# Feed-forward weights in alternating pieces, loaded one piece further ahead, with the low parts of the first layer formed on GpSimd

## The chip, the core and the metric

The kernel runs on one core of a Trainium2 chip. The metric is device time in microseconds (us). In the rows PE is TensorE's matmul, PEld its weight load, DVE VectorE, ACT ScalarE, POOL GpSimd, and SP SyncE, which only issues transfers.

## The reference: what is computed

An mLSTM recurrence over 768 steps for 4 batches of 8 sequences with head dimension 40, then a feed-forward layer in two matrix products with a piecewise activation between them:

```python
m_new = np.maximum(f_gate[:, :, t] + m, i_gate[:, :, t])        # per step t
f_stab = np.exp(f_gate[:, :, t] + m - m_new); i_stab = np.exp(i_gate[:, :, t] - m_new)
C = f_stab * C + i_stab * outer(v_t, k_t);  n = f_stab * n + i_stab * k_t
y[:, :, t] = sigmoid(o_gate_t) * (C @ q_t) / np.maximum(np.abs(n . q_t), 1.0)
# x: 3072 tokens x 320, the y of all batches and steps
h = x @ w_in                                                     # 320 x 2048
g = np.where(h >= 1, h, np.where(h <= -1, 0.0, (h + 1) ** 2 / 4))
out = g @ w_out                                                  # 2048 x 320
```

## The kernel before

The 768 steps are cut into 6 chunks of 128, so there are 24 heads of work n = 0 to 23 (a chunk of one batch, 8 sequences at once). Four heads make a group of 512 tokens. The feed-forward layer goes over six groups j = 0 to 5, and in each over 16 pieces fc of 128 of the 2048 inner features; call x = 16 j + fc the number of such a piece. `mm1(j, fc)` makes h of a piece in one bank `psh` (8 matmuls of 512 columns: high parts xh, wh against low parts xl, wl, since a product in fp32r keeps fewer bits), ScalarE and VectorE form r = g(h), and `mm2` multiplies r into four banks `pso`, two pieces (LAG) later. There are two `psh` banks, so mm1(x) cannot start before r of x-2 has been taken out of its bank.

While the layer runs over one group, the heads of the next are computed between its pieces: `prep` (select of the decay matrix Abc on GpSimd, its exponentials on ScalarE, v scaled by gates on GpSimd), `score` (products `psa<-raw`, multiplied into Abc on VectorE), `main` (products `psa<-C,qn` and `psa<-v,Abc`, the sums hv, the quotients z, sz and y on VectorE, `carry_on` with products `psa<-v,vk` for the next state C, a transposition `psa<-ident,y`, and the copies xh on ScalarE and xl, xh on VectorE that mm1 of the next group needs). The heads 0 to 3 go first, in a front part whose order is written out by hand in `STEPS`; their own `carry_on` (products `psa<-ow`, from v that GpSimd has scaled) follows during group 0.

The weights come as int64 words of float64 values and are converted during group 0. Each layer has 8 pieces, in_0 to in_7 and out_0 to out_7, each good for two values of fc. `load_w` brings one into a raw buffer `wraw` (transfers are all issued by SyncE, in order). `convert` runs `words` (mg on ScalarE; mg, the sign bits and the joining SCALAR_TENSOR_TENSOR on VectorE; the low half words on GpSimd) and, for in_i, `split`: wh on ScalarE (a cast), then wl = win - wh on VectorE. out_i is used as plain fp32 in group 0 (`pso<-ow,r`) and split in group 1 only. `win`, the converted piece of w_in, has one buffer.

What sets the order: `W_ORDER` lists the pieces, `DUE(fc)` says how many of them are converted by piece fc, `split_next` converts one, behind the instructions marked ("x", "act") and ("x", "dve"), which are the copies xh and xl of the last head done so far, and then loads the piece two places on. All else in this part is placed by the framework's scheduler, which follows these marks, the order in the program and the buffers; each engine then runs its list strictly in order.

Of the kernel before, what the change touches and what calls it, by code (L numbers as in the profile page):

```python
# [31 lines left out]

LAG = 2

PLAIN_FC = 16

# [10 lines left out]


GATES_AT = 34
DUE = lambda fc: 3 + fc

STEPS = (
# [3 lines left out]
)  # L61
# [37 lines left out]
def mlstm_ffn_kernel(ctx, tc, qk, qn, vk, og, fi0, fi, fib, w_in, w_out, cst, out):  # L99
    nc = Core(tc)  # L100
# [80 lines left out]
    mb = {}  # L181

    def load_batch():
        mb["row"] = mid.tile([NSEQ, 2, 4 * L], F32, name="fi_r")
        nc.sync.dma_start(mb["row"], fi[:, :, L:5 * L])
        mb["fi"] = mid.tile([P, 2, L], F32, name="fi_b")
        nc.sync.dma_start(mb["fi"], fib)
# [10 lines left out]

    def batch_sums():
        a, m = mb["fi"][:, 0, :], mb["m"]  # L200
        ah = mb["ah"] = mid.tile([P, L], F32, name="ah_b")
        ac = mb["ac"] = mid.tile([P, L], F32, name="ac_b")
        nc.vector.tensor_tensor(out=a, in0=a, in1=m[:, :L], op=ALU.add)
        nc.vector.tensor_tensor(out=a, in0=a, in1=m[:, 1:], op=ALU.subtract)
        nc.vector.tensor_scalar(out=ah, in0=a, scalar1=CLAMP, scalar2=GRID, op0=ALU.max, op1=ALU.add)
        nc.vector.tensor_scalar(out=ah, in0=ah, scalar1=-GRID, scalar2=None, op0=ALU.add)
        nc.vector.tensor_tensor_scan(out=ac, data0=rst, data1=ah, initial=0.0, op0=ALU.mult, op1=ALU.add)
        nc.sync.dma_start(a_d[1:5].rearrange("c s t -> (c s) t"), ac)
        nc.vector.scalar_tensor_tensor(out=a, in0=a, scalar=CLAMP, in1=ah, op0=ALU.max, op1=ALU.subtract)
# [160 lines left out]
    ol = {}  # L370
# [18 lines left out]
        nc.vector.scalar_tensor_tensor(out=out, in0=mg.bitcast(I32), scalar=3, in1=out,  # L389
                                       op0=ALU.logical_shift_left, op1=ALU.bitwise_or)  # L390

    def split(hi, lo, w):
        nc.scalar.copy(hi, w)
        yield
        nc.vector.tensor_tensor(out=lo, in0=w, in1=hi.bitcast(F32), op=ALU.subtract)

    raws = {}

    def load_w(kind, i):
        if kind == "in":  # L400
            n = 2 * P
            raw = stage.tile([P, 3, 2 * n], I32, name="wraw", bufs=2)
            at = nc.sync.dma_start(raw.rearrange("p k f -> p (k f)"), w_in[i])
        else:
            raw = stage.tile([P, 2, 2 * DM], I32, name="wraw", bufs=2)
            at = nc.sync.dma_start(raw.rearrange("p k f -> p (k f)"), w_out[i])
        raws[kind, i] = raw
        return at

    def convert(kind, i):  # L410
        raw = raws.pop((kind, i))
        if kind == "in":
            sl = slice(2 * i * P, 2 * (i + 1) * P)
            w = stage.tile([P, 3, 2 * P], F32, name="win", bufs=1)
            words(w, raw)
            yield
            yield from split(wh[:, :, sl], wl[:, :, sl], w)
        else:
            of[i] = ow.tile([P, 656], F32, name="ow")[:, :2 * DM].rearrange("p (k e) -> p k e", k=2)
            words(of[i], raw)  # L420
            if 2 * i >= PLAIN_FC:
                yield
                yield from split_out(i)

    def split_out(i):
        w = of.pop(i)
        ol[i] = ow.tile([P, 656], F32R, name="ow")[:, :2 * DM].rearrange("p (k e) -> p k e", k=2)
        yield from split(oh[:, 2 * i:2 * i + 2, :], ol[i], w)


    W_ORDER = [("in", 0)]
    for i in range(NFC // 2):
        if i + 1 < NFC // 2:
            W_ORDER.append(("in", i + 1))
        W_ORDER.append(("out", i))


    front = True
# [274 lines left out]
    for n in range(NS):  # L713
        j, r = divmod(n, NTC)
# [87 lines left out]
    for what in STEPS.split():  # L802
        n = int(what[1]) if what[1:2].isdigit() else 0
        hh = int(what[2:] or 0)
        if what == "Lg":
            first_gates()
        elif what == "Lf":
            load_batch()
        elif what == "Lc":
            nc.sync.dma_start(cs_t, cst[0:120, P:])  # L810
        elif what == "Li":
            nc.sync.dma_start(ident, cst[:, :P])
        elif what == "Lo":
            load_og(0)
        elif what[:2] == "Lq":
            load_qk(hh)
        elif what[:2] == "Lv":
            load_v2(hh)
        elif what[:2] == "Lw":
            mark["load"] = load_w(*W_ORDER[hh])  # L820
        elif what[0] == "s":
            score_mm(n)
        elif what[0] == "m":
            score_mul(n, hh)
        elif what[0] == "g":
            if n:
                batch_sums()
            else:
                run(gate_sums(n))
        elif what[0] == "b":  # L830
            batch_maxima()
        elif what[0] == "k":
            run(gate_tail(n))
        elif what[0] == "h":
            gate_exps(n)
        elif what[0] == "A":
            add_sums(n)
        elif what[0] == "E":
            exponents(n)
        elif what[0] == "p":  # L840
            first_sums()
        elif what[0] == "v":
            scale1(n)
        elif what[0] == "o":
            sigmoid(0)
        elif what[0] == "x":
            decay(n, hh)
        elif what[0] == "c":
            rest = convert(*W_ORDER[nw])
# [29 lines left out]
    for x in range(NG + LAG):  # L879
        j, fc = divmod(x, NFC)  # L880
        if x < NG:
            if j == 0:
                while nw < min(len(W_ORDER), DUE(fc)):
                    split_next()
                if nw == len(W_ORDER) and late is None:
                    stages.close()
                    late = ctx.enter_context(tc.tile_pool(name="late", bufs=1, side="right"))
            if fc == 0:
                ops[j] = [ps_o.tile([P, 512], F32, name="pso") for _ in range(NTC)]
            if j == 1 and fc % 2 == 0 and fc < PLAIN_FC:  # L890
                with tc.issue_after(mark["r", "act"].ins), tc.issue_after(mark["r", "dve"].ins):
                    for _ in split_out(fc // 2):
                        pass
            if x == GATES_AT:
                load_gates(later, NC - 1, NC)
                steps = gate_steps(NC - 1)
            if x >= GATES_AT:
                with tc.issue_after(mark["r", "dve"].ins):
                    next(steps, None)
            r = mm1(j, fc)  # L900
            if x == 0:
                with tc.issue_after(mark["r", "dve"].ins):
# [68 lines left out]
```

## Time and profile before

| | us |
|---|---|
| time, median of 3 runs (518.02 to 518.27) | 518.25 |
| span of the profiled execution, first to last instruction | 516.2 |
| time outside the span (median less span) | 2.05 |
| TensorE busy in the span | 490.7 |
| VectorE, ScalarE, GpSimd busy | 343.0, 289.1, 135.9 |
| mean granted TensorE clock | 0.979 |

The profiled execution is one of its own, with no device time noted beside its span; the difference of 2.05 us to the median is taken as what lies around the span. Group 0 runs in it from 33.6 us, when mm1(0) starts, to 143.0 us, when mm1(16) starts. From 160 us to the end TensorE is nearly always busy. A row of a view by stretches gives, for each engine, its busy time and in brackets its number of instructions; then the granted clock (1.00 is full, 0.50 half), the busy share of the transfer engines and what they moved. A busy time of TensorE at half clock is still busy: the loss stands in the column of the clock.

### The profile page before, as it was taken

Reading aid. Unit: us, or ns where it says so; the run is one execution under the profiler, and the core shown is the slowest. Engines: PE = TensorE matmul, PEld = TensorE weight load, DVE = VectorE, ACT = ScalarE, POOL = GpSimd, SP = SyncE. Lnnn points to the kernel's source line nnn. Section 1 sums busy time; section 2 is a strip of 40 time slices with the busy share of each in tenths; the row PEclk is TensorE's granted clock in tenths of the full one; section 3 lists DMA queues with packets and bytes.
Section 4 is the critical chain, followed back from the end, with each engine's and each line's share of the span. In section 5 each row is a group of like instructions: output and inputs, shape, how many; then the busy total and the mean of one; then the engine's idle time right before and its main releaser. Section 6 shows DMA issues by size and latency. Waiting matters only on the chain.

```text
span 516.2 us, 8817 instructions
## 1 busy us (share of the span) xinstructions
PE 490.7 (95%) x3396; PEld 419.4 (81%) x3399; DVE 343.0 (66%) x621; ACT 289.1 (56%) x560; POOL 135.9 (26%) x136
## 2 busy tenths in 40 slices
PE   8985999889898999999999998999999999999996
PEld 3763877778677989988889988889888889988986
DVE  4789896679758776759696657756756745444332
ACT  4525884436087555676645567555377554455553
POOL 2324531343433333323142314403230210000000
PEclk8987999979999999999999999999999999999999
DMA  8868664364441303323223423113522000010001
GB/s 227 257 183 307 161 189 138 115 193 150 131 146 40 107 27 96 118 66 111 65 78 83 133 80 118 68 53 96 170 81 77 16 1 1 0 52 1 1 2 51
DMA packets 29646, 51.48 MB, mean 100 GB/s; under 512 B 10060, under 2 KB 19940, under 8 KB 29604
## 3 DMA queue, kind: packets, MB, share of 16 engines
q1 hardware_dynamic: 29604, 50.92, 32.4%
q8 instruction: 27, 0.44, 0.4%
q14 instruction: 15, 0.12, 0.1%
HBM read 46.80 MB, written 4.04 MB: 98 GB/s over the span
## 4 chain that ended last, share of the span: by engine, by line
PE 85%; DVE 6%; ACT 5%; DMA 3%; issue 1%; SPq 0%; ACTq 0%; DVEq 0%
PE pso L82 33%; PE psh L82 33%; PE psa L82 15%; ACT Abc L82 1%; PE pso L85 1%; DMA raw<-in_qk 1%; ACT L82 1%; PE psa L85 1%; DVE ow L82 1%; DMA wraw<-in_w_in 1%; PE psh L85 1%; ACT r L82 1%; DVE win L82 1%; DMA out<-r 1%; ACT sig L82 0%
## 5 line engine op out<-in xcount | busy, mean ns | idle before, releaser
L82 ACT ACTIVATE r<-psh,half 128x512 f32<-128x512 f32 x96 | 65.4, 685 | 111.7 <-PE psh L82 111.4
L82 DVE SCALAR_TENSOR_TENSOR r<-psh,r 128x512 f32<-128x512 f32 x96 | 65.8, 686 | 71.5 <-ACT r L82 71.3
L82 PE MATMUL psh<-xh,wh 128*128 128x512 f32 x288 | 104.3, 418 | 6.7 <-DVE r L82 6.1
L82 PE MATMUL pso<-oh,gh 128*128 128x320 f32 x320 | 100.6, 317 | 2.4 <-ACT gh L82 2.1
L82 PE MATMUL psh<-xh,wl 128*128 128x512 f32 x288 | 99.8, 401 | 0.0
L82 PE MATMUL pso<-ow,gh 128*128 128x320 f32 x320 | 99.2, 312 | 0.0
L82 PE MATMUL pso<-oh,gl 128*128 128x320 f32 x320 | 94.0, 311 | 1.6 <-DVE gl L82 1.6
L82 DVE TENSOR_TENSOR gl<-r,gh 128x512 fp32r<-128x512 f32 x80 | 62.2, 779 | 40.5 <-ACT gh L82 40.4
L82 ACT CAST gh<-r 128x512 fp32r<-128x512 f32 x80 | 49.4, 618 | 51.0 <-DVE r L82 50.4
L82 PEld LDWEIGHTS pso<-oh,gh 128*128 128x128 f32 x320 | 60.1, 188 | 7.4 <-ACT gh L82 2.5
L82 PEld LDWEIGHTS psh<-xh,wl 128*128 128x128 f32 x288 | 55.2, 192 | 13.1 <-DVE wl L85 0.4
L82 PEld LDWEIGHTS psh<-xh,wh 128*128 128x128 f32 x288 | 51.8, 194 | 15.2 <-DVE r L82 6.8
L82 PEld LDWEIGHTS pso<-ow,gh 128*128 128x128 f32 x320 | 60.2, 188 | 2.8
L82 PE MATMUL psh<-xl,wh 128*128 128x512 f32 x192 | 62.3, 405 | 0.0
L82 ACT ACTIVATE r<-r 128x512 f32<-128x512 f32 x96 | 60.4, 632 | 2.5
L82 PEld LDWEIGHTS pso<-oh,gl 128*128 128x128 f32 x320 | 58.9, 188 | 2.1 <-DVE gl L82 1.9
L82 ACT ACTIVATE Abc<-Abc,nA 128x128 f32<-128x128 f32 x160 | 49.9, 391 | 0.2
L82 POOL TENSOR_TENSOR v<-vk,G 128x328 f32<-128x328 f32 x36 | 30.6, 856 | 58.3 <-issue 45.9
L82 PEld LDWEIGHTS psh<-xl,wh 128*128 128x128 f32 x192 | 36.8, 192 | 8.6
L82 PE MATMUL pso<-ow,r 128*128 128x320 f32 x128 | 38.5, 443 | 0.5 <-DVE ow L82 0.5
L82 POOL TENSOR_SCALAR_AFFINE_SELECT Abc<-Abc 128x1024 f32<-128x1024 f32 x20 | 25.4, 1275 | 48.3 <-DMA Abc<-a_d 46.1
L82 POOL TENSOR_TENSOR m<-m 128x1024 bf16<-128x1024 f32 x12 | 24.4, 2037 | 46.4 <-DVE m L82 46.4
(203 smaller groups left out, 681.0 us busy)
## 6 DMA issues: line engine op xcount, KB each, us to landing
Abc<-a_d SPq DMA_DIRECT2D x20, 512.0 KB
raw<-in_qk SPq DMA_DIRECT2D x48, 160.0 KB
vk<-in_vk SPq DMA_DIRECT2D x20, 324.0 KB
wraw<-in_w_in SPq DMA_DIRECT2D x8, 768.0 KB
wraw<-in_w_out SPq DMA_DIRECT2D x8, 640.0 KB
sig<-in_og SPq DMA_DIRECT2D x6, 640.0 KB
out<-r SPq DMA_DIRECT2D x24, 160.0 KB
qn<-in_qn SPq DMA_DIRECT2D x20, 180.0 KB
```

Source lines behind the costliest of these rows:

```text
L82: r = getattr(self.engine, name)(*args, **kwargs)
L85: r = getattr(self.engine, name)(*args, **kwargs)
```

## The change

Seven things change.

1. `W_ORDER` is in_0, out_0, in_1, out_1 and so on. Before it was in_0, in_1, out_0, in_2, out_1, ..., with the first layer one piece further ahead.
2. The raw buffers are three instead of two, and a conversion loads the piece three places on.
3. A new step Lw2 in the hand-written front loads the third piece, in_1, right after the constants `cs`. The two before it are in_0 and out_0 (before: in_0 and in_1), and the step c then loads out_1 (before: out_0).
4. wl is formed on GpSimd instead of VectorE (`split` takes the engine).
5. Only two pieces are converted ahead of mm1(0) instead of three. The later ones are converted after mm1 of their fc and behind the marks of r instead of those of xh and xl, with `DUE` one higher from fc = 1 on.
6. The tiles ah and ac of the gate sums for the chunks 1 to 4 lie in the space of the row buffer `fi_r`, which makes room for the third raw buffer.
7. `PLAIN_FC`, which was 16 (all pieces), is gone with the branches that it switched.

```diff
-DUE = lambda fc: 3 + fc
+DUE = lambda fc: 3 + fc + (fc > 0)
 STEPS = (
-    "Lg Li Lo Lq0 Lv0 Lq1 Lw0 Lf Lq2 Lv2 Lq3 Lw1 Lc o w9 E0 ...
+    "Lg Li Lo Lq0 Lv0 Lq1 Lw0 Lf Lq2 Lv2 Lq3 Lw1 Lc Lw2 o w9 E0 ...
...
-        mb["row"] = mid.tile([NSEQ, 2, 4 * L], F32, name="fi_r")
+        mb["all"] = mid.tile([P, 2, 4 * L], F32, name="fi_r")
+        mb["row"] = mb["all"][:NSEQ]
...
-        ah = mb["ah"] = mid.tile([P, L], F32, name="ah_b")
-        ac = mb["ac"] = mid.tile([P, L], F32, name="ac_b")
+        ah = mb["ah"] = mb["all"][:, 0, :L]
+        ac = mb["ac"] = mb["all"][:, 0, L:2 * L]
...
-    def split(hi, lo, w):
+    def split(hi, lo, w, eng):
         nc.scalar.copy(hi, w)
         yield
-        nc.vector.tensor_tensor(out=lo, in0=w, in1=hi.bitcast(F32), op=ALU.subtract)
+        eng.tensor_tensor(out=lo, in0=w, in1=hi.bitcast(F32), op=ALU.subtract)
...
-            raw = stage.tile([P, 3, 2 * n], I32, name="wraw", bufs=2)
+            raw = stage.tile([P, 3, 2 * n], I32, name="wraw", bufs=3)
...
-            yield from split(wh[:, :, sl], wl[:, :, sl], w)
+            yield from split(wh[:, :, sl], wl[:, :, sl], w, nc.gpsimd)
...
-    W_ORDER = [("in", 0)]
-    for i in range(NFC // 2):
-        if i + 1 < NFC // 2:
-            W_ORDER.append(("in", i + 1))
-        W_ORDER.append(("out", i))
+    W_ORDER = [(kind, i) for i in range(NFC // 2) for kind in ("in", "out")]
...
-            if nw + 2 < len(W_ORDER):
-                load_w(*W_ORDER[nw + 2])
+            if nw + 3 < len(W_ORDER):
+                load_w(*W_ORDER[nw + 3])
...
-                while nw < min(len(W_ORDER), DUE(fc)):
+                while nw < 2:
                     split_next()
...
             r = mm1(j, fc)
...
+            while j == 0 and nw < min(len(W_ORDER), DUE(fc)):
+                split_next("r")
```

How this moves the instructions is not to be seen in the diff. Three places follow; the number behind a name tells buffers apart, and only their order counts.

First, the transfers that SyncE issues in the front. `wraw` is a raw weight piece, `vk`, `qn` and `raw` (qk) belong to the heads 4 and 5, `m_b` carries the row maxima to the gate sums, and `Abc` is the decay matrix of a head, read back from `a_d`. Before:

```order
L85 DMA wraw_161<-in_w_in 128x1536
L85 DMA cs_99<-in_cst 120x369
L82 DMA vk_493<-in_vk 128x648
L82 DMA qn_495<-in_qn 120x384
L82 DMA raw_497<-in_qk 40x1024 x2
L82 DMA vk_661<-in_vk 128x648
L82 DMA raw_500<-in_qk 40x1024 x2
L85 DMA wraw_284<-in_w_out 128x1280
L82 DMA qn_663<-in_qn 120x384
L82 DMA fi_t_2430<-in_fi 32x2x128
L85 DMA m_b_302<-m_r_298 32x129 x4
```

And with the change:

```order
L84 DMA wraw_161<-in_w_out 128x1280
L84 DMA cs_99<-in_cst 120x369
L84 DMA wraw_164<-in_w_in 128x1536
L81 DMA vk_493<-in_vk 128x648
L81 DMA qn_495<-in_qn 120x384
L81 DMA raw_497<-in_qk 40x1024 x2
L81 DMA raw_500<-in_qk 40x1024 x2
L84 DMA wraw_286<-in_w_out 128x1280
L81 DMA vk_670<-in_vk 128x648
L81 DMA qn_672<-in_qn 120x384
L81 DMA fi_t_2428<-in_fi 32x2x128
L84 DMA m_b_304<-m_r_300 32x129 x4
```

So out_0 comes in the place of in_1, in_1 right behind it, and out_1 in the place of out_0: one piece more stands ahead of `m_b`.

Second, GpSimd from the first piece of w_in on. AFFINE_SELECT is the select of Abc (heads 4 to 6), `ow_581` and `ow_630` are the v of the heads 0 and 1, scaled for their `carry_on`, and `v1`, `v2` those of head 4. Before:

```order
L82 TENSOR_TENSOR ow_581<-ow_581,G_121 128x328
L82 TENSOR_TENSOR ow_621<-ow_621,G_121 128x328
L82 TENSOR_SCALAR win_591<-wraw_522 128x768
L82 TENSOR_SCALAR ow_628<-wraw_531 128x640
L82 AFFINE_SELECT Abc_503<-Abc_503 128x1024
L82 AFFINE_SELECT Abc_505<-Abc_505 128x1024
L82 AFFINE_SELECT Abc_507<-Abc_507 128x1024
L82 TENSOR_SCALAR win_676<-wraw_600 128x768
```

With the change (`win_570` is in_1, `win_613` in_2):

```order
L81 TENSOR_TENSOR ow_581<-ow_581,G_121 128x328
L81 AFFINE_SELECT Abc_503<-Abc_503 128x1024
L81 TENSOR_TENSOR wl_132<-win_570,wh_131 128x3x256
L81 AFFINE_SELECT Abc_505<-Abc_505 128x1024
L81 AFFINE_SELECT Abc_507<-Abc_507 128x1024
L81 TENSOR_SCALAR win_613<-wraw_520 128x768
L81 TENSOR_SCALAR ow_650<-wraw_579 128x640
L81 TENSOR_TENSOR v1_668<-vk_493,G_121 128x328
L81 TENSOR_TENSOR v2_769<-vk_493,G_121 128x328
L81 TENSOR_TENSOR ow_630<-ow_630,G_121 128x328
L81 TENSOR_TENSOR wl_132<-win_613,wh_131 128x3x256
```

The wl of in_1 now stands behind the first select, and the scaling for head 1's `carry_on`, which stood ahead of all three selects (as `ow_621`), stands behind them and five more. On TensorE `psa_659<-ow_630`, the products of that `carry_on`, come right ahead of mm1(4) (`psh_740`), where before they came behind mm1(4).

Third, VectorE when the first heads of the next group end. Before, head 4's xl and xh (`xl_978`, `xh_977`) and head 5's hv, z, sz and y (`hv_986` and on):

```order
L82 TENSOR_TENSOR xl_978<-psa_973,xh_977 128x2x128
L82 TENSOR_TENSOR xh_977<-psa_973,xh_977 64x128
L82 TENSOR_SCALAR win_1010<-wraw_895 128x768
L82 TENSOR_SCALAR ow_1071<-wraw_955 128x640
L82 TENSOR_TENSOR hv_986<-psa_982,G_121 128x328
L82 TENSOR_SCALAR mg_1011<-mg_1011 128x768
L82 SCALAR_TENSOR_TENSOR win_1010<-mg_1011,win_1010 128x768
L82 TENSOR_TENSOR hv_986<-psa_988,hv_986 128x328
L82 SCALAR_TENSOR_TENSOR z_1048<-hv_986,G_121 128x8
L82 TENSOR_TENSOR z_1048<-z_1048,hv_986 128x8
L82 TENSOR_TENSOR wl_132<-win_1010,wh_131 128x3x256
```

With the change (head 4's are `xl_987`, `xh_986`, head 5's `hv_995` and on):

```order
L81 TENSOR_TENSOR xl_987<-psa_982,xh_986 128x2x128
L81 TENSOR_TENSOR xh_986<-psa_982,xh_986 64x128
L81 SCALAR_TENSOR_TENSOR r_1330<-psh_1321,r_1330 128x512
L81 TENSOR_TENSOR ow_1349<-ow_513,oh_133 128x640
L81 TENSOR_TENSOR hv_995<-psa_991,G_121 128x328
L81 TENSOR_TENSOR hv_995<-psa_997,hv_995 128x328
L81 SCALAR_TENSOR_TENSOR z_1057<-hv_995,G_121 128x8
L81 TENSOR_TENSOR z_1057<-z_1057,hv_995 128x8
L81 RECIPROCAL z_1057<-z_1057 128x8
L81 TENSOR_TENSOR sz_1061<-sig_491,z_1057 128x320
L81 TENSOR_TENSOR y_1063<-hv_995,sz_1061 128x320
```

The conversions of in_6 (`win_1010`), in_7, out_6 and out_7 no longer stand between the steps of the heads 5 to 7: the last one, of out_7, comes ahead of head 4's xl. `r_1330` is that of mm1(15). So with the change all 16 mm1 of group 0 stand ahead of head 5's end, while before mm1(12) to mm1(15) stood behind the mains of heads 4 and 5 (12 and 13) and of head 6 (14 and 15).

More of the change, by code (lines that the diff above doesn't have):

```diff
@@ L33 @@
 LAG = 2
-PLAIN_FC = 16
 FRONT = 22
@@ L401, in load_w @@
             n = 2 * P
-            raw = stage.tile([P, 3, 2 * n], I32, name="wraw", bufs=2)
+            raw = stage.tile([P, 3, 2 * n], I32, name="wraw", bufs=3)
             at = nc.sync.dma_start(raw.rearrange("p k f -> p (k f)"), w_in[i])
         else:
-            raw = stage.tile([P, 2, 2 * DM], I32, name="wraw", bufs=2)
+            raw = stage.tile([P, 2, 2 * DM], I32, name="wraw", bufs=3)
             at = nc.sync.dma_start(raw.rearrange("p k f -> p (k f)"), w_out[i])
@@ L420, in convert @@
             words(of[i], raw)
-            if 2 * i >= PLAIN_FC:
-                yield
-                yield from split_out(i)
     def split_out(i):
@@ L427, in split_out @@
         ol[i] = ow.tile([P, 656], F32R, name="ow")[:, :2 * DM].rearrange("p (k e) -> p k e", k=2)
-        yield from split(oh[:, 2 * i:2 * i + 2, :], ol[i], w)
-    W_ORDER = [("in", 0)]
-    for i in range(NFC // 2):
-        if i + 1 < NFC // 2:
-            W_ORDER.append(("in", i + 1))
-        W_ORDER.append(("out", i))
+        yield from split(oh[:, 2 * i:2 * i + 2, :], ol[i], w, nc.vector)
+    W_ORDER = [(kind, i) for i in range(NFC // 2) for kind in ("in", "out")]
     front = True
@@ L850, in mlstm_ffn_kernel @@
             next(rest)
-            load_w(*W_ORDER[nw + 2])
+            load_w(*W_ORDER[nw + 3])
             nw += 1
@@ L889, in mlstm_ffn_kernel @@
                 ops[j] = [ps_o.tile([P, 512], F32, name="pso") for _ in range(NTC)]
-            if j == 1 and fc % 2 == 0 and fc < PLAIN_FC:
+            if j == 1 and fc % 2 == 0:
                 with tc.issue_after(mark["r", "act"].ins), tc.issue_after(mark["r", "dve"].ins):
@@ L904, in mlstm_ffn_kernel @@
                     batch_exps()
+            while j == 0 and nw < min(len(W_ORDER), DUE(fc)):
+                split_next("r")
             with behind(("v", "pool")):
                 slot(FRONT + x)
-            gs[x] = parts(r) if j or fc >= PLAIN_FC else (r,)
+            gs[x] = parts(r) if j else (r,)
         if x >= LAG:
```

2 rows, old and new, of the table STEPS are left out of this document.

## The prediction

> **What bounds the kernel now.** I read the stretches first, from mm1(0) to the end. Columns: length, then PE, PEld, DVE, ACT and POOL busy, granted clock, share and rate of the transfers.
>
> ```profile
> 33.00:67.00 34.00, 27.31 (x114) 20.49 (x116) 30.63 (x47) 21.44 (x46) 17.52 (x16) 0.85 0.78 230
> 67.00:97.00 30.00, 30.00 (x150) 22.85 (x148) 20.66 (x33) 16.47 (x26) 7.35 (x8) 1.00 0.45 150
> 97.00:112.00 15.00, 11.86 (x73) 9.76 (x72) 12.40 (x23) 6.04 (x13) 5.67 (x6) 0.77 0.65 206
> 112.00:130.00 18.00, 18.00 (x93) 14.36 (x92) 13.93 (x24) 11.07 (x21) 6.42 (x7) 1.00 0.38 117
> 130.00:143.00 13.00, 11.08 (x73) 8.68 (x72) 10.45 (x19) 1.86 (x5) 5.18 (x5) 1.00 0.47 143
> 160.00:506.00 346.00, 343.72 (x2536) 306.67 (x2535) 219.68 (x394) 198.46 (x375) 77.21 (x69) 1.00 0.21 63
> ```
>
> From 160 us on TensorE is busy 343.72 of 346.00 at full clock: nothing of this change reaches there, and a gain before it only moves that part forward. In group 0 TensorE is not always the bound. From 33 to 67 it is idle 6.7 us and the clock takes 0.15 x 34 = 5.1 more (some counted twice). From 97 to 112 it is idle 3.1 and the clock takes 0.23 x 15 = 3.4, from 130 to 143 it is idle 1.9: together **8.4 us lost late**. Between these stretches it waits for nothing. The waits view of TensorE from 33 to 150 us says for whom:
>
> ```profile
> PE psh L82 <- DVE r L82: 6.1, 1, 6.1
> PE psa L82 <- DVE hv L82: 2.4, 2, 1.8
> PE psa L82 <- DVE xh L82: 1.3, 2, 0.8
> ```
>
> The early loss is one wait for VectorE's r of mm1(0). The late ones are the heads' own steps on VectorE. The shorter stretches show what such a wait does to the clock:
>
> ```profile
> 45.00:49.00 4.00, 3.80 (x9) 3.02 (x10) 3.96 (x12) 0.60 (x2) 1.85 (x2) 0.50 1.00 311
> 104.00:106.00 2.00, 0.24 (x2) 0.05 (x1) 1.93 (x4) 0.42 (x1) 0.73 (x1) 0.78 0.78 261
> 106.00:108.00 2.00, 1.99 (x14) 1.77 (x14) 1.89 (x6) 1.11 (x2) 0.05 (x1) 0.50 0.90 353
> ```
>
> After a wait of 1.8 us (104 to 106) the clock stands at half. The 0.77 of the row from 97 to 112 is a loss of 3.4 us, so the half clock lasts 6.8 us.
>
> **The late part.** What VectorE does in that wait stands in the timeline: win, mg and the joining of in_6 lie between head 5's two hv, because the conversions follow the marks of xh and xl.
>
> ```profile
> 101.76 0.97 DVE L82 TENSOR_SCALAR win<-wraw 128x768 uint16<-128x768 uint16 x1
> 103.17 0.50 DVE L82 TENSOR_TENSOR hv<-psa,G 128x328 f32<-128x328 f32 x1
> 104.18 1.37 DVE L82 SCALAR_TENSOR_TENSOR win<-mg,win 128x768 int32<-128x768 int32 x1
> 105.47 0.49 DVE L82 TENSOR_TENSOR hv<-psa,hv 128x328 f32<-128x328 f32 x1
> 106.01 2.07 PE L82 MATMUL psa<-raw 40*128 40x128 f32 x14 [1.77 <-DVE hv L82]
> ```
>
> With the change the conversions follow r, and all are done before the heads 5 to 7 finish. For this to gain, TensorE must be kept busy by mm1 and mm2 from about mm1(6) on, and the heads, which now come last, must not lose as much. The durations are in the groups by shape, 30 to 145 us (busy, mean ns | idle before):
>
> ```profile
> L82 PE MATMUL psa<-raw 40*128 40x128 f32 x80 | 8.6, 317 | 1.8 <-DVE hv L82 1.8
> L82 PE MATMUL psa<-v,Abc 128*128 128x41 f32 x64 | 7.7, 281 | 1.3 <-DVE xh L82 1.3
> L82 DVE SCALAR_TENSOR_TENSOR r<-psh,r 128x512 f32<-128x512 f32 x16 | 10.8, 681 | 9.2 <-ACT r L82 9.2
> L82 ACT ACTIVATE r<-psh,half 128x512 f32<-128x512 f32 x16 | 10.8, 679 | 23.2 <-PE psh L82 23.1
> L82 DVE SCALAR_TENSOR_TENSOR ow<-mg,ow 128x640 int32<-128x640 int32 x8 | 9.9, 1237 | 0.2
> L82 DVE SCALAR_TENSOR_TENSOR win<-mg,win 128x768 int32<-128x768 int32 x7 | 8.6, 1226 | 0.2
> L82 DVE TENSOR_SCALAR win<-wraw 128x768 uint16<-128x768 uint16 x7 | 6.9, 981 | 0.2
> L82 DVE TENSOR_TENSOR wl<-win,wh 128x768 fp32r<-128x768 f32 x7 | 7.4, 1058 | 0.9 <-ACT wh L82 0.8
> L82 ACT CAST wh<-win 128x768 fp32r<-128x768 f32 x7 | 5.8, 827 | 12.9 <-DVE win L82 12.9
> L82 POOL TENSOR_SCALAR win<-wraw 128x768 uint16<-128x768 uint16 x7 | 8.9, 1271 | 20.3 <-DVE mg L82 7.4 <-DVE wl L82 7.4 <-DMA wraw<-in_w_in 3.3
> L82 POOL TENSOR_SCALAR_AFFINE_SELECT Abc<-Abc 128x1024 f32<-128x1024 f32 x7 | 9.0, 1302 | 8.0 <-DMA Abc<-a_d 8.0
> L82 POOL TENSOR_TENSOR v<-vk,G 128x328 f32<-128x328 f32 x10 | 8.6, 866 | 9.6 <-PE psa L82 6.3 <-issue 2.0 <-ACT G L82 1.2
> L82 POOL TENSOR_TENSOR ow<-ow,G 128x328 f32<-128x328 f32 x4 | 4.3, 1068 | 0.6 <-DMA ow<-in_vk 0.5
> L82 DVE TENSOR_TENSOR hv<-psa,hv 128x328 f32<-128x328 f32 x4 | 2.0, 494 | 1.3 <-PE psa L82 1.3
> L82 DVE TENSOR_TENSOR y<-hv,sz 128x320 f32<-128x320 f32 x4 | 2.2, 562 | 0.1
> ```
>
> and the chain of waits gives a piece on TensorE at full clock:
>
> ```profile
> 76.89 1.86 PE psh L82 x8
> 78.75 2.15 PE pso L82 x8
> ```
>
> A pair of pieces (one in, one out) costs TensorE 2 x (1.86 + 2.15) = 8.0 us, and with the heads' scores and products between them about 10. VectorE's share of the pair is two r (1.36), win and its joining (0.98 + 1.23), the joining of ow (1.24) and three smaller ones of at most 0.98 each: under 7.8. The chain that feeds the next mm1 is joining, wh, relu and r: 1.23 + 0.83 + 0.68 + 0.68, with a square like the relu (0.68) 4.1 us, and it has two pieces of time. So from mm1(6) to mm1(15) I expect **no wait of TensorE**: the cover is its own 8 to 10 us per pair. If a wait of 0.5 us appeared at each of these ten, 5 us would go.
>
> Then the heads 5 to 7 remain, with only the last mm2 beside them. Call T the end of head 5's `psa<-v,Abc`. TensorE still has 1.75 mm2 (3.8), head 7's scores (1.2), and for each head C,qn (1.0, estimated from 0.8 to 1.0 between neighbours in the trace), v,Abc (7.7/4 = 1.9), v,vk (0.8) and a transposition (0.5; both estimates too). Between v,Abc and the transposition VectorE does hv 0.49, two z, reciprocal and sz (estimated at 1.35 together), and y 0.56: 2.4 us, of which v,vk and, for head 7, head 8's scores cover 0.8 and 2.0. Head 5's is covered wholly by the mm2. So TensorE waits 1.6 us for head 6's y and 0.4 for head 7's. **Late: 8.4 becomes 2.0, a gain of 6.4 us**; 8.4 if the heads wait for nothing, about 0 if each waits as now. One bound below: a wait of 1.6 us is close to the 1.8 that halved the clock at 106. If it does so for 6.8 us, 3.4 us go.
>
> The Trainium skill, TensorE: Matmul & The Clock Gate, section "What's actually happening", says that the clock is halved only after an idle window of about 3.4 us. The trace halves it after 1.8 us idle in 2.0, so the rule as stated is too mild here. By the rule head 6's wait costs only itself, by the row it may cost those 3.4 us more.
>
> **The early part.** VectorE loses its wl of in_0 (1.06 in the mean) and does not wait for in_1 before r of mm1(0): ahead of r stand now only the conversion of out_0 and the gate sums. These rows carry it:
>
> ```profile
> 35.18 0.28 DVE L85 TENSOR_TENSOR fi_b<-fi_b,m_b 128x128 f32<-128x128 f32 x1
> 37.64 0.81 DVE L85 TENSOR_TENSOR fi_b<-fi_b,m_b 128x128 f32<-128x128 f32 x1
> 48.06 3.94 POOL L82 TENSOR_SCALAR_AFFINE_SELECT Abc<-Abc 128x1024 f32<-128x1024 f32 x3 [1.66 <-DMA Abc<-a_d]
> 44.46 0.69 DVE L82 SCALAR_TENSOR_TENSOR r<-psh,r 128x512 f32<-128x512 f32 x1
> 56.61 0.46 PEld L82 LDWEIGHTS psh<-xh,wh 128*128 128x128 f32 x2
> ```
>
> r comes at about 39 instead of 44.46, and mm2(0) fills part of the old 6.1 us. But mm1(2) needs wh of in_1, whose conversion now stands behind that r: joined at about 43, wh at 44, against a start near 45 before (the row from 45 to 49 has TensorE busy again). Its wl and head 1's scaled v then queue on GpSimd. Before, Abc lands at 48.06, when the select starts. Now `a_d` is written some 2 us sooner (an estimate from the gate sums, which stand behind one conversion instead of two), and out_1 no longer stands ahead of Abc (0.66 MB, 2.1 us at the 311 GB/s of 45 to 49), so I put Abc near 44. From there GpSimd does three selects (3.9), wl (1.8), low words of in_2 and out_2 (1.27, and 1.06 for 640 of 768), v twice (1.7) and ow once (1.07): 10.8, so `ow_630` is ready at 55. TensorE stands at its products ahead of mm1(4). On VectorE the copy of that state into C (estimated at 0.5) stands ahead of r of mm1(2), so mm1(4) starts near 56.5, against 56.61 before. TensorE has then the products of head 1 (0.4) more done, and has idled 4 us just before, so the clock is halved as it was. **Early: 0 to -0.5 us; I take -0.4.** The ends: +4 if GpSimd's list gets through 4 us sooner (Abc at 41), -4 if Abc lands at 48 as now.
>
> The new wl on GpSimd is not in the trace. Its nearest rows, two-input ones of 328 elements at 0.87 (`v<-vk,G`), give 2.0 for 768, the select's 1.30 for 1024 with one input gives 1.0; I take 1.8, near the two-input end. Eight wl take 14 us from GpSimd's idle time and give VectorE back 8.4. VectorE can lose them again: fi_b took 0.81 instead of 0.28 while GpSimd worked beside it. The Trainium skill, SBUF — State Buffer, section "SBUF: two separate sides", says why: one port pair is held for a whole instruction, by GpSimd or by a VectorE instruction with two SBUF inputs, and the other is blocked. The 0.81 agrees. By that rule eight wl could hold VectorE up to 14 us, more than it is relieved of; VectorE busy only 20.66 of 30.00 from 67 to 97 is what hides it.
>
> The third raw piece in the front (0.66 MB ahead of m_b) fits the transfers' own gap: they moved 59 GB/s at a share of 0.37 from 31 to 34 us.
>
> ```profile
> 31.00:34.00 3.00, 1.15 (x5) 0.75 (x5) 2.36 (x8) 1.22 (x3) 0.91 (x1) 0.91 0.37 59
> ```
>
> If it did not, m_b and VectorE's gate sums behind it would come up to 2.1 us later (at 311 GB/s), which the GpSimd chain would pass on. The shared space of `fi_r` and the dropped `PLAIN_FC` move no work.
>
> **The sum.** Span 516.2 - 6.4 + 0.4 = 510.2, and with the 2.05 us outside it **512.2 us**.
>
> **Rivals.** A, the early wait goes too: GpSimd's list is faster than I think (for it: in_2's low words and out_2's need not wait for transfers; against it: Abc's landing in the trace is late). 3 to 4 us and part of the half clock: 508. B, the late waits only move: heads 5 to 7 at the end have no more mm1 beside them, and each y is awaited as hv was, so the 8.4 stay: 518.5. For it speak the same VectorE steps of 2.4 us, against it that no conversion stands between them. C, slower: wl on GpSimd, behind its selects and scalings and stretched by VectorE's two-input work, ends later than the 2.15 us of mm2 that stand between mm1's wh part and its wl part. This decides from the point at which wl takes over 2.2 us after wh. Then in_3 to in_7 wait about 1 us each, and two of the waits halve the clock for 6.8 us as at 106: 5 + 6.8 on top of the forecast: 524. The lock rule above would lead here; GpSimd's 7.35 of 30.00 busy from 67 to 97 speaks against it.
>
> **How the numbers follow.** Forecast 0.50, own range 510 to 515.6 (the clock at head 6); A 0.18; B 0.20; C 0.12. The range leaves out C and the better part of A: 507.5 to 519. A measurement tells 0.2%, about 1 us, from no change. Faster: the forecast, A and a quarter of B, 0.74; same: half of B, 0.10; slower: C and the rest of B, 0.16.
>
> **What would show it.** Right: mm1(6) still near 66 us, no wait of TensorE over 0.3 us and clock 1.00 from there to head 5, mm1(16) near 137 instead of 143, waits for y at the end of group 0, wl on POOL near 1.8 us. Wrong: a wait of `psh` for POOL wl after mm1(6) (C), waits for hv and y of 8 us together (B), or mm1(4) well before 56 (A).

## The result, and the profile after

The changed kernel takes **525.57 us** (median of 4, 523.97 to 525.75) against 518.13 before on the same chip: ratio **1.0138**, 95% interval 1.0118 to 1.0159. It is slower. The forecast was 512.2, with a range of 507.5 to 519.0.

The view by stretches of the changed kernel, in the stretches that the prediction used (length, then PE, PEld, DVE, ACT and POOL busy with the number of instructions, granted clock, share and rate of the transfers):

```profile
33.00:67.00 34.00, 25.98 (x91) 18.68 (x91) 20.30 (x40) 20.07 (x42) 19.31 (x17) 0.81 0.74 225
67.00:97.00 30.00, 30.00 (x146) 22.53 (x144) 24.31 (x32) 20.04 (x31) 13.87 (x11) 1.00 0.50 167
97.00:112.00 15.00, 15.00 (x83) 11.64 (x82) 12.82 (x19) 9.12 (x17) 4.61 (x4) 1.00 0.22 70
112.00:130.00 18.00, 16.96 (x100) 13.13 (x99) 8.93 (x19) 4.20 (x9) 4.11 (x5) 1.00 0.25 78
130.00:143.00 13.00, 9.89 (x56) 9.22 (x55) 7.20 (x19) 2.42 (x8) 4.88 (x6) 0.68 0.43 122
143.00:160.00 17.00, 14.81 (x115) 12.22 (x115) 10.60 (x23) 8.78 (x17) 6.13 (x6) 0.74 0.57 182
```

The stretch that lost 3.1 us of idle time and the half clock before, 97 to 112, is now full at clock 1.00, as forecast. The others are worse. From 112 to 130 TensorE is idle 1.0 us where it was never idle; from 130 to 160 it is idle 5.3 us, and the clock stands at 0.68 and 0.74. From 33 to 67 it is idle 8.0 us, against 6.7.

The waits of TensorE from 33 to 160 us in the changed kernel (us in total, times, longest):

```profile
PE psa L81 <- POOL ow L81: 4.7, 1, 4.7
PE psa L81 <- DVE y L81: 2.3, 1, 2.3
PE psh L81 <- POOL wl L81: 1.7, 1, 1.7
PE psa L81 <- DVE C L81: 1.5, 2, 1.2
PE psh L81 <- DVE r L81: 1.2, 1, 1.2
PE psa L81 <- DVE Abc L81: 1.1, 2, 0.7
PE psa L81 <- DVE xh L81: 0.8, 2, 0.5
```

The first, third and fifth lie before 57 us; y, C, Abc and xh are the heads 5 to 7 at the end of group 0. Of the kernel before's waits, the 6.1 us for r early and the 2.4 for hv late have shrunk to 1.2 and 0.6; those for ow, y, wl and C are new in this size.

To compare kernels I use one measure, the **loss**: the idle time of TensorE, plus the busy time multiplied by what the granted clock lacks of 1.00, added up over stretches of half a microsecond. Nothing is counted twice. Span less loss is 481 to 484 us in every kernel of this study but e4, which has added work (491), so the differences in time are differences in loss. By stretch:

| loss, us | 0 to 32 | 32 to 67 | 67 to 97 | 97 to 177 | 177 to end | span |
|---|---|---|---|---|---|---|
| before | 5.5 | 11.5 | 0 | 10.8 | 6.5 | 516.2 |
| after | 4.7 | 13.5 | 0 | 15.6 | 7.1 | 524.0 |

Of the 7.8 us between the spans 4.8 arose from 97 to 177, 2.1 from 32 to 67.

What happens at the end is in the timeline of TensorE. Head 4's products come behind mm1(12) (the first matmuls of mm1(12) stand at 96.92), and all pieces are done by 127 us:

```profile
98.72 1.92 PE L81 MATMUL psa<-v,Abc 128*128 128x41 f32 x16
132.60 0.87 PE L81 MATMUL psa<-v,vk 128*120 128x123 f32 x6
135.82 0.87 PE L81 MATMUL psa<-ident,y 128*128 128x128 f32 x3 [2.35 <-DVE y L81]
138.12 3.61 PE L81 MATMUL psa<-v,Abc 128*128 128x41 f32 x16 [0.22 <-DVE xh L81]
145.03 2.07 PE L81 MATMUL psa<-raw 40*128 40x128 f32 x14 [1.22 <-DVE C L81]
149.38 1.20 PE L81 MATMUL psh<-xh,wh 128*128 128x512 f32 x2
```

In the kernel before, the same products of head 4 stood at 90.14, behind mm1(10):

```profile
90.14 1.92 PE L82 MATMUL psa<-v,Abc 128*128 128x41 f32 x16
```

So from there on the heads 5, 6 and 7 have nothing beside them but each other. Each is a chain that crosses from TensorE to VectorE and back several times, and most crossings now leave TensorE waiting. mm1(16), which needs the last head, starts at 149.4 instead of 143.0.

### The profile page after: what moved, and what is told of

It reads as the page before. It is cut to its first block, busy times and chain, and to the rows that moved or that the text cites. A ratio compares the mean times of both kernels' runs of the same rounds, so it can differ in the third digit from the quotient of the medians.

```text
span 524.0 us, 8832 instructions
## 1 busy us (share of the span) xinstructions
PE 495.7 (95%) x3399; PEld 423.5 (81%) x3399; DVE 334.9 (64%) x613; ACT 289.8 (55%) x560; POOL 146.9 (28%) x144
## 4 chain that ended last, share of the span: by engine, by line
PE 78%; DMA 7%; ACT 6%; DVE 4%; issue 2%; POOL 1%; SPq 1%; ACTq 0%; POOLq 0%; DVEq 0%
PE pso L81 32%; PE psh L81 31%; PE psa L81 15%; ACT L81 2%; DMA wraw<-in_w_in 2%; DMA raw<-in_qk 2%; ACT r L81 1%; DMA wraw<-in_w_out 1%; ACT Abc L81 1%; ACT sig L81 1%; DMA m_b<-m_r 1%; DMA a_d<-fi_r 1%; DMA Abc<-a_d 1%; SPq L84 1%; DVE z L81 0%
## 5 line engine op out<-in xcount | busy, mean ns | idle before, releaser
L81 PE MATMUL psh<-xh,wl 128*128 128x512 f32 x288 | 100.9, 403 | 1.7 <-POOL wl L81 1.7
L81 PE MATMUL pso<-ow,r 128*128 128x320 f32 x128 | 40.0, 455 | 0.2 <-DVE r L81 0.2
L81 POOL TENSOR_SCALAR_AFFINE_SELECT Abc<-Abc 128x1024 f32<-128x1024 f32 x20 | 23.8, 1193 | 54.8 <-DMA Abc<-a_d 49.9
```

What stands on the lines that cost most here:

```text
L81: r = getattr(self.engine, name)(*args, **kwargs)
```

## Experiments

All kernels compute the whole result. Times are medians; a ratio is against the kernel before on the same chip. The word "ahead" below means: so many of the 16 mm1 of group 0 have begun on TensorE when head 4's `psa<-v,Abc` starts (11 before, 13 after).

### e1: the marks of the heads again

```diff
-                split_next("r")
+                split_next("x")
```

> The changed kernel with one thing undone: its conversions stand again behind the marks of the heads (xh, xl) instead of behind those of r. Theory T (the loss is at the end of group 0: all 16 mm1 run ahead of the heads 5 to 7, which then wait for VectorE with nothing beside them, idle 5.7 us and 5.9 us at half clock between 125 and 149 us): mm1(12) to mm1(15) stand between the heads again, the late loss falls from 11.7 us to 4 to 6, the time to 518 to 520. Rival P (GpSimd's longer list is the loss, through the 4.7 us wait for ow ahead of mm1(4) and late wl): nothing of it is undone here, 524 to 526.

Measured: 517.82 us, ratio 0.9973 (0.9941 to 1.0005). The loss from 97 to 177 is 5.3 us instead of 15.6, with no half clock in it; early it is 15.1, 1.5 more than with the change. The waits of TensorE from 97 to 177 us:

```profile
PE pso L81 <- DVE gl L81: 1.6, 1, 1.6
PE psh L81 <- POOL wl L81: 1.4, 1, 1.4
PE psa L81 <- DVE hv L81: 0.6, 1, 0.6
PE psa L81 <- DVE Abc L81: 0.6, 1, 0.6
```

The waits for y, C and xh are gone, and the interval includes 1: with the marks of the heads put back, the other six changes together neither gain nor lose clear of the noise. The loss sits at the end, as theory T said. But more moved than T named: not only do mm1(14) and mm1(15) stand behind head 6's products again, head 4's products also came forward, to 81.6 us with 8 ahead. Which of the two counts was open.

### e2: wl on VectorE again

```diff
-            yield from split(wh[:, :, sl], wl[:, :, sl], w, nc.gpsimd)
+            yield from split(wh[:, :, sl], wl[:, :, sl], w, nc.vector)
```

> The changed kernel with wl formed on VectorE again, all else as changed. Theory T: the end of group 0 keeps its order, the late loss stays 11 to 12 us; the GpSimd list ahead of ow_630 is one wl (1.8 us) shorter, so mm1(4) starts 1 to 2 us sooner: 523 to 525. Rival P: with wl off GpSimd the time is back at 518 to 519.

Measured: 524.02 us, ratio 1.0099 (1.0071 to 1.0127). Early the loss falls from 13.5 to 9.8 us, late it rises from 15.6 to 18.2; the order at the end is unchanged (13 ahead). GpSimd's list is thus not the main cause: rival P falls.

### e3: the kernel before, with only wl on GpSimd

```diff
-        nc.vector.tensor_tensor(out=lo, in0=w, in1=hi.bitcast(F32), op=ALU.subtract)
+        (nc.gpsimd if w.shape[1] == 3 else nc.vector).tensor_tensor(out=lo, in0=w, ...)
```

> The kernel before with only wl of w_in moved to GpSimd. Theory T: the order of pieces and heads late stays about as before, VectorE is relieved by 7 to 8 us, no new waits: 516 to 519. Rival P: wl late on GpSimd costs waits of TensorE in group 0, 521 to 525.

Measured: 517.66 us, ratio 0.9971 (0.9945 to 0.9997), barely told from no change. Moving wl costs nothing in itself. It also gains next to nothing, though eight wl, 8.4 us in all, leave VectorE. The busy times of the pages, first the kernel before, then e3:

```profile
PE 490.7 (95%) x3396; PEld 419.4 (81%) x3399; DVE 343.0 (66%) x621; ACT 289.1 (56%) x560; POOL 135.9 (26%) x136
```

```profile
PE 492.5 (95%) x3399; PEld 420.9 (82%) x3399; DVE 344.1 (67%) x613; ACT 289.0 (56%) x560; POOL 150.4 (29%) x144
```

VectorE has 8 instructions fewer and is busy 1.1 us longer: what it was relieved of came back in the length of its other instructions. That holds for this order of the instructions, not for every one. The changed kernel and e2 also differ in the engine of wl alone, and there VectorE is busy 4.5 us less with wl on GpSimd; first the changed kernel, then e2:

```profile
PE 495.7 (95%) x3399; PEld 423.5 (81%) x3399; DVE 334.9 (64%) x613; ACT 289.8 (55%) x560; POOL 146.9 (28%) x144
```

```profile
PE 495.5 (95%) x3399; PEld 423.6 (81%) x3399; DVE 339.4 (65%) x621; ACT 289.5 (56%) x560; POOL 134.0 (26%) x136
```

### e4: filling TensorE at the end

```diff
         hot(xp)
+        if n in (6, 7):
+            for _ in range(16):
+                nc.tensor.matmul(xp[:, :P], ident, ident, start=True, stop=True)
```

> The changed kernel with 16 products of the identity with itself (thrown away) put on TensorE ahead of the transpositions of y of the heads 6 and 7, where it waits for y. They add 2 x 1.8 us of work at full clock, nothing else. Theory T with the clock as its larger half: the granted clock stays at 1.00 through the end of group 0 and 5 to 6 us come back, of which 0 to 2 go for the added work: 520 to 522. If the half clock there comes from something else than the idle time (the kind of work, for one), it stays and the added work costs 2 to 7 us at the clock it gets: 526 to 532.

Measured: 531.43 us, ratio 1.0231 (1.0163 to 1.0300), inside the second expectation. I had the price wrong: 16 such products show as 32 records and take 3.84 us at full clock, twice my 1.8, and 6.16 in the second place, most of it at half clock. The first filling did hold the clock at the place where it fell in the changed kernel (134.7 us); it fell at 141.3 instead, after the next waits. The stretches of e4:

```profile
131.20:134.50 3.30, 3.30 (x31) 3.22 (x30) 1.62 (x4) 0.84 (x3) 1.52 (x3) 1.00 0.44 146
134.60:137.90 3.30, 3.30 (x32) 3.30 (x31) 2.11 (x5) 0.22 (x1) 1.07 (x1) 1.00 0.58 192
138.00:141.30 3.30, 2.51 (x23) 2.38 (x23) 1.47 (x4) 0.15 (x1) 0.95 (x2) 1.00 0.19 56
141.40:144.70 3.30, 1.76 (x9) 1.25 (x10) 3.13 (x9) 0.00 (x0) 1.22 (x2) 0.50 0.59 177
```

Neither expectation is clean: the half clock does follow the waits, but covering one wait does not pay when the next follows within 4 us.

### e5: the marks of the heads for the last five conversions only

```diff
-                split_next("r")
+                split_next("r" if fc < 10 else "x")
```

> The changed kernel with the marks of the heads for the conversions at fc = 10 and later only (out_5, in_6, out_6, in_7, out_7); the early part is the change's own. Theory T (at the end of group 0 the heads 5 to 7 stand bare, because all 16 mm1 run ahead of them): mm1(14) and mm1(15) stand after head 6's products again, the wait of 2.3 us for y and the half clock from 135 to 152 us go, the late loss falls from 11.7 us to 4 to 8, the early one stays: 518 to 522. If the place of these conversions does nothing for the end: 524 to 526.

Measured: 525.38 us, ratio 1.0133 (1.0086 to 1.0180). A miss. mm1(14) and mm1(15) do stand behind head 6's products, and the half clock is shorter, but 13 mm1 are still ahead of head 4, the wait for y is still 2.0 us, and one for wh of the held conversions (1.8) joins it: late loss 14.1. In the narrower stretch that the expectation had in mind, 125 to 149.5 us, the loss did fall, from 11.7 to 7.9 us, but 2.3 us are now lost before it, and the time did not follow. So the place of the last two pieces alone is not the cause. **Theory T falls in this form.** What e1 had and e5 has not is the early place of head 4.

### e6: head 1's v ahead of two selects

```diff
+        with behind(*([("ow", 1)] if n in (5, 6) else [])):
             nc.gpsimd.affine_select(out=A, in_=A, ...)
```

Here `mark["ow", n]` is the scaling of v in `scale2`.

> The changed kernel with one thing moved on GpSimd: the selects of Abc of the heads 5 and 6 stand behind the scaling of v of head 1 (ow_630). Theory T2 (the 4.7 us wait ahead of mm1(4) is GpSimd's list and nothing else): ow_630 is ready 2.5 us sooner (two selects of 1.25), mm1(4) starts at 54 to 55 instead of 56.98, the half clock there stays or is shorter by one stretch of 3.4 us: 521 to 524. If the load of head 1's v sets it (issued at 41.4 us), mm1(4) stays at 56 to 57 and the time at 524 to 526.

Measured: 523.01 us, ratio 1.0078 (1.0057 to 1.0099). mm1(4) starts at 55.83 instead of 56.98. The wait for ow falls from 4.7 to 3.0, not by the 2.5 I named, and the wait for wl rises from 1.7 to 2.7. The early loss falls from 13.5 to 11.5 us: that part of the early wait is GpSimd's list, and the late loss stays at 15.4.

### e7 and e8: both ends, with wl on either engine

```diff
-ST = 0
+ST = -2
...
-                split_next("r")
+                split_next("x")
```

ST is the place in the plan at which the `carry_on` of the heads 0 to 3 begins; it makes the states that the heads 4 to 7, the next chunk of the same batches, start from. e8 has the edit of e2 as well.

> A version meant to join both: the changed kernel with the marks of the heads for all conversions (as in e1) and the carry_on of the heads 0 to 3 two places sooner in the plan, by which the products of head 1 and mm1(4) no longer stand behind GpSimd's v of head 2. Theory: the late loss stays at 4 to 6 us as in e1, and of the early loss of 15.1 us in e1 the wait of 4.6 and half of the half clock go, 7 us: 508 to 513. If the early wait only moves to another instruction: 515 to 519 as e1.

> As e7 with wl on VectorE. Theory: GpSimd's list is 1.8 us shorter per piece, VectorE's 1.06 longer; the late end has VectorE on its path again, 0 to 3 us dearer there, the early part 0 to 2 us cheaper than e7: 508 to 516. If wl on GpSimd is what carries the gain of e1: 517 or more.

Measured: e7 525.50 us, ratio 1.0145 (1.0085 to 1.0204); e8 **510.90 us, ratio 0.9856 (0.9822 to 0.9890)**, the fastest of all and faster than both kernels. e7 is a miss. Between the two only the engine of wl differs in the code, but the order differs too: in e7 10 mm1 are ahead and the late loss is 12.6, in e8 8 and 4.2. Besides, e7 loses 5.3 us from 67 to 97, where one wait of 3.6 us for r is followed by 3.4 us at half clock, and e8 1.6. The waits of TensorE in e8 from 97 to 152 us:

```profile
PE pso L81 <- DVE r L81: 0.6, 1, 0.6
PE psa L81 <- DVE hv L81: 0.6, 1, 0.6
PE psa L81 <- DVE Abc L81: 0.6, 1, 0.6
PE pso L81 <- ACT gh L81: 0.5, 1, 0.5
```

This gave theory T3: what is lost late depends on how many pieces stand ahead of head 4's products, since the heads that follow need those pieces as cover.

### e9 and e10: only the place of the heads

e9 is the changed kernel with `ST = -2` and nothing else; e10 has wl on VectorE too. Both keep the marks of r.

> The changed kernel with one number altered: the carry_on of the heads 0 to 3 stands two places sooner in the plan, marks of r, wl on GpSimd and all else as changed. By this head 4's main (its products C,qn and v,Abc) stands ahead of mm1(7) instead of behind mm1(12). Theory T3 (the late loss is what the pieces take from the heads' cover when they run ahead of head 4's main; it was 16 us from 97 to 177 us with 13 pieces ahead, 13 with 9 or 10, 4 to 5 with 8): the late loss falls to 4 to 6 us though the conversions keep the marks of r; the early loss stays at 13 to 15 (the products of head 2 and the scores stand ahead of mm1(4)): 513 to 517. If the marks of the heads on the conversions are what saved e1 and e8: late loss 11 or more, 521 to 526.

> As e9 with wl on VectorE as well. Theory T3: late loss 4 to 6 us as in e9, early loss about 9 as in e8 (9.8 in e2), since GpSimd's list is short and only head 1's products stand ahead of mm1(4): 509 to 513. If the marks of the heads matter: 520 or more.

Measured: e9 515.33 us, ratio 0.9947 (0.9923 to 0.9971); e10 512.34 us, ratio 0.9899 (0.9880 to 0.9917). Both times lie in T3's ranges. Head 4's products start at 81.4 us with 7 ahead in e9, at 74.0 with 8 in e10. The late loss falls from 15.6 us to 8.8 in e9 and, against e2, from 18.2 to 8.7 in e10 (4 to 6 was expected). One number, in a place of the program that touches no conversion, turns the change from 1.4% slower to 0.5% faster. Not all of that is late: the early loss falls too, from 13.5 to 8.8 us in e9, with the wait for `ow` (4.7 us) gone. (In the profiled execution of e9 the clock stood at half from 8.8 to 32.7 us, in no other for so long in the front, so its span of 520.1 us is not used, only its part from 32 us on; e10's, without that, has the same late loss.) What is left late in e10, TensorE's waits from 97 to 177:

```profile
PE psa L81 <- DVE C L81: 2.3, 1, 2.3
PE pso L81 <- DVE gl L81: 1.7, 1, 1.7
```

The wait for C, head 7's state ahead of the last scores (132.8 us), brings 3.2 us of half clock with it.

### e11: the same number in the kernel before

```diff
-ST = 0
+ST = -2
```

> The kernel before with the same one number altered; its conversions keep their order and the marks of the heads. Head 4's main stands behind mm1(8) instead of mm1(10). Theory T3: the late loss falls from 10.8 us to about 6 to 9, the early one stays near 10.5: 512 to 517. If the gain of e8 needs the new order of the pieces: 517 to 520.

Measured: 515.64 us, ratio 0.9951 (0.9927 to 0.9975). The time is in T3's range, the way to it is not. The late loss is 12.5 us with 9 ahead, not 6 to 9 and more than the 10.8 before; the gain came early, where the loss fell from 11.5 to 7.9.

### e12: e8 without the shift

```diff
-                split_next("r")
+                split_next("x")
...
-            yield from split(wh[:, :, sl], wl[:, :, sl], w, nc.gpsimd)
+            yield from split(wh[:, :, sl], wl[:, :, sl], w, nc.vector)
```

> e8 without the shift of the carry_on: the changed kernel with the marks of the heads on the conversions and wl on VectorE. Head 4's main stands ahead of mm1(8), as in e1 and e8. Theory T3 with both parts (the place of head 4's main and the marks of the heads): late loss 4 to 6 us; early loss between e8 (8.9) and e1 (15.1), since the products of head 2 stand ahead of mm1(4) but GpSimd has no wl ahead of them: 511 to 515. If it is the shift that carries e8: 516 or more.

Measured: 518.22 us, ratio 0.9992 (0.9956 to 1.0028). A miss of T3; the second expectation, that the shift carries e8, is the one that came true, for only ST differs between the two. The early loss is 9.0 as foreseen and 8 mm1 are ahead, but the late loss is 7.9, and 4.6 more are lost from 67 to 97, where one wait for hv halved the clock from 82.0 to 88.8 us:

```profile
82.47 0.79 PE L81 MATMUL psa<-raw 40*128 40x128 f32 x2 [1.50 <-DVE hv L81]
```

### All of them together

Loss in us from the profiled executions (e4 has work added):

| kernel | ahead of head 4 | loss 97 to 177 | loss 32 to 67 | wl on | time, us |
|---|---|---|---|---|---|
| e9 | 7 | 8.8 | 8.8 | GpSimd | 515.33 |
| e8 | 8 | 4.2 | 8.9 | VectorE | 510.90 |
| e1 | 8 | 5.3 | 15.1 | GpSimd | 517.82 |
| e12 | 8 | 7.9 | 9.0 | VectorE | 518.22 |
| e10 | 8 | 8.7 | 8.6 | VectorE | 512.34 |
| e11 | 9 | 12.5 | 7.9 | VectorE | 515.64 |
| e7 | 10 | 12.6 | 10.1 | GpSimd | 525.50 |
| e3 | 10 | 12.8 | 10.5 | GpSimd | 517.66 |
| before | 11 | 10.8 | 11.5 | VectorE | 518.13 |
| e4 | 13 | 11.3 | 13.6 | GpSimd | 531.43 |
| e5 | 13 | 14.1 | 13.6 | GpSimd | 525.38 |
| e6 | 13 | 15.4 | 11.5 | GpSimd | 523.01 |
| after | 13 | 15.6 | 13.5 | GpSimd | 525.57 |
| e2 | 13 | 18.2 | 9.8 | VectorE | 524.02 |

With up to 8 ahead the late loss is 4 to 9 us, with 9 to 11 it is 11 to 13, with 13 it is 14 to 18 (e4's filling aside). That is a tendency over kernels that differ in more than this. Five pairs differ in ST alone, 0 against -2:

| pair | marks, wl on | ahead | loss 97 to 177 | loss 32 to 67 | time, us |
|---|---|---|---|---|---|
| after, e9 | r, GpSimd | 13, 7 | 15.6, 8.8 | 13.5, 8.8 | 525.57, 515.33 |
| e2, e10 | r, VectorE | 13, 8 | 18.2, 8.7 | 9.8, 8.6 | 524.02, 512.34 |
| e1, e7 | heads, GpSimd | 8, 10 | 5.3, 12.6 | 15.1, 10.1 | 517.82, 525.50 |
| e12, e8 | heads, VectorE | 8, 8 | 7.9, 4.2 | 9.0, 8.9 | 518.22, 510.90 |
| before, e11 | heads, VectorE | 11, 9 | 10.8, 12.5 | 11.5, 7.9 | 518.13, 515.64 |

In the first three the late loss goes with the number ahead, in e1 and e7 upward, for there the same shift put more pieces ahead. In the last two it does not: between e12 and e8 it falls from 7.9 to 4.2 with 8 ahead in both, and between the kernel before and e11 it rises though the number falls. So T3 holds for what the change lost, 13 pieces ahead against 7 or 8, and not as a rule that the number alone sets the loss.

**Open:** the order of the pieces and the third raw buffer were not undone alone. e10 against e11, both with the shift and wl on VectorE, differ by what is left of the change, and e10 is faster (intervals 0.9880 to 0.9917 and 0.9927 to 0.9975), so that rest is no loss once the heads stand early. Why e7 and e12 lose 5.3 and 4.6 us from 67 to 97 where e9 and e10 lose none was not followed further, nor why the same shift moved head 4 forward in some kernels and back in e7.

## Why the prediction was wrong

**What bounds the kernel: right.** Everything is decided in group 0. From 160 to 506 TensorE is busy 341.37 us against 343.72:

```profile
160.00:506.00 346.00, 341.37 (x2525) 304.22 (x2525) 222.19 (x395) 201.92 (x386) 80.69 (x72) 1.00 0.21 66
```

Of the 2.4 us between these two, 2.2 are the same pair of waits of mm2 for gh and gl, which lies before 160 us in the kernel before and between 162 and 167 now.

**No wait from mm1(6) on: right.** TensorE is idle 0.00 us from 67 to 125, and mm1(6) starts at 67.8 us (near 66 was forecast).

**"Late: 8.4 becomes 2.0": the step that failed.** From 125 to 149.4 us the loss is 11.7: idle 5.7, half clock 5.9. Three terms of that step were off. The wait for head 6's y was put at 1.6 and is 2.35. The waits for C, xh and Abc (1.2 and 0.3, 0.5 and 0.2, 0.7 and 0.4: 3.4 in all) were not in the sum, for I had counted only the way from v,Abc to the transposition and left out the state C, which the next head's C,qn and the last scores wait for. The half clock stood outside the sum as a bound of 3.4 us and cost 5.9 there, and 1.2 more after 149.4. The larger mistake is behind these terms: I took the pieces that run ahead as a gain. They are the heads' cover. e9 and e10 show it for this change: with the heads forward by one number, the same marks and pieces lose 8.8 instead of 15.6 us late, and 8.7 instead of 18.2. e1 shows it from the other side: with the marks of the heads back, 8 pieces are ahead and 5.3 us are lost.

Part of the 2.35 is a short VectorE instruction that was held up. The timeline of VectorE for head 6, and the same instruction for head 7 without GpSimd beside it:

```profile
132.81 0.50 DVE L81 TENSOR_TENSOR hv<-psa,hv 128x328 f32<-128x328 f32 x1 [1.60 <-PE psa L81]
133.70 0.68 DVE L81 TENSOR_TENSOR z<-z,hv 128x8 f32<-128x8 f32 x1
135.18 0.49 DVE L81 TENSOR_TENSOR y<-hv,sz 128x320 f32<-128x320 f32 x1
142.65 0.17 DVE L81 TENSOR_TENSOR z<-z,hv 128x8 f32<-128x8 f32 x1
```

GpSimd at that moment:

```profile
132.91 1.45 POOL L81 TENSOR_TENSOR v<-vk,G 128x328 f32<-128x328 f32 x2 [1.74 <-PE psa L81]
```

z on 8 elements takes 0.68 us and ends at 134.38, when GpSimd's scaling ends (132.91 + 1.45 = 134.36).

**"Early: 0 to -0.5 us": nearly right in the start of mm1(4), wrong in what follows.** `ow_630` was ready at 54.1 us (55 forecast), mm1(4) started at 56.98 (56.5). But before, the half clock was over by 51 us, and mm1(4) ran at full clock; now the wait of 4.7 us halves it from 52.8 to 63.0, and mm1(4) and an mm2 run through 6 us of that at half. I had written that the clock is halved "as it was". The loss from 32 to 67 is 13.5 instead of 11.5 us. e2 and e6 show that it hangs on GpSimd's list: 3.7 us less with wl off it, 2.0 less with two selects behind `ow_630`. The sum also had the sign of this term against its own working: mm1(4) 0.1 us sooner with 0.4 us more work done is a gain of 0.5 us, and 0.4 was added. Beside a miss of 13 us that is nothing. (The chances have a like slip: their parts come to 0.73 faster and 0.17 slower, not 0.74 and 0.16.)

**wl on GpSimd, 1.8 us: right**, 1.83 in the mean of the groups by shape:

```profile
L81 POOL TENSOR_TENSOR wl<-win,wh 128x768 fp32r<-128x768 f32 x7 | 12.8, 1831 | 18.3 <-ACT wh L81 18.3
```

That VectorE gets 8.4 us back is right for the whole change, with VectorE busy 334.9 instead of 343.0 us, but not as the worth of moving wl: that was 4.5 us here (against e2), and less than nothing in e3. The prediction named this possibility and hid it behind VectorE's slack from 67 to 97; there TensorE indeed lost nothing.

**The rivals.** B had the place right (the waits only move to the heads 5 to 7) and the size too small: it let the 8.4 us stay, for 518.5, with a chance of 0.20. C gave nearly the measured time, 524, but that is luck: its mechanism did not occur, for after mm1(6) TensorE never waits for wl. A did not occur either.

## What to carry to other kernels

When two streams share an engine and one is a chain of short crossings, work of the other that runs ahead is cover spent: count for the last steps of the chain what still stands beside them, before counting a removed wait as gain. When an edit loosens an order, look for the place of the *other* stream: here a shift of its start by two places, in one number, decided between 525 and 515 us. Read the new order before trusting such a shift, though: with the marks of e1 the same number cost 8 us (e7). And a wait can cost the clock that follows it on top of its length, wherever it is moved to: a wait of 1.5 us did in e12, one of 1.6 us in e1 did not.

## What was not expected of the hardware

**A busy TensorE can keep the clock down.** In the changed kernel the clock fell at 134.7 us and came back only at 151.7. Three of its stretches:

```profile
131.50:134.80 3.30, 1.98 (x18) 1.79 (x17) 1.85 (x5) 0.44 (x2) 1.45 (x2) 0.98 0.51 140
138.30:141.60 3.30, 3.30 (x17) 3.30 (x17) 0.20 (x1) 0.00 (x0) 0.49 (x1) 0.50 0.21 56
141.70:145.00 3.30, 2.11 (x9) 1.60 (x8) 3.06 (x8) 0.00 (x0) 1.68 (x2) 0.50 0.63 171
```

From 138.3 to 141.6 TensorE is busy 3.30 of 3.30 us, and the clock stays at half in the next stretch. Its work there is head 7's `psa<-v,Abc`, products of 41 columns. And in e4 the clock fell after a stretch in which TensorE was busy 2.51 of 3.30 us (138.0 to 141.3, with such products in it), but not after this one, with less:

```profile
127.70:131.10 3.40, 2.26 (x17) 1.93 (x17) 2.80 (x7) 1.88 (x7) 1.36 (x2) 1.00 0.57 154
```

So busy time as the profile records it does not decide, and the kind of work seems to count; that it is the narrow products is an inference from these stretches, not a run of its own. The Trainium skill, TensorE: Matmul & The Clock Gate, section "What's actually happening", has the clock fall after an idle window of about 3.4 us and rise after a busy one. The length fits (the half clock here lasts 17.1 us, five times 3.4); "idle" and "busy" as this profile counts them do not.

**Work moved from VectorE to GpSimd may not relieve VectorE.** In e3 8.4 us were moved, and VectorE was busy 1.1 us longer. In the changed kernel against e2 it was relieved by 4.5 us, in e7 against e8 it was busy 2.7 us longer (342.6 against 339.9); in each of these pairs the engine of wl is the only edit. The row of VectorE that grew most from the kernel before (first line) to e3 (second line) is this (instructions, busy us and mean ns of one, idle before them):

```profile
L82 DVE TENSOR_SCALAR mg<-mg 128x640 f32<-128x640 f32 x8 | 3.8, 480 | 0.0
L82 DVE TENSOR_SCALAR mg<-mg 128x640 f32<-128x640 f32 x8 | 7.0, 872 | 2.1 <-ACT mg L82 2.1
```

The Trainium skill, SBUF — State Buffer, section "SBUF: two separate sides", tells of one port pair that GpSimd, or a VectorE instruction in a two-port mode or with two SBUF inputs, holds whole; z at 0.68 instead of 0.17 us, ending with GpSimd's instruction, agrees. Whether the mg rows grew by the same lock was not followed.
